# A half of a down projection done at the end of its own group, or at the start of the next

## The chip, the cores and the metric

The kernel runs on one core of one Trainium2 chip. The metric is the device time of one execution in microseconds (us). The kernel before took 368.73 us, the median of three runs (368.56 to 369.21). All times below are from these runs and from one profiled execution of the same kernel.

## The reference, cut to what matters

```python
# gated linear attention, 4 batches x 8 heads x 768 tokens x 48
for t in range(S):
    state = alpha[t][:, None] * state + k[t] (outer) v[t]
    y[t] = q[t] @ state
x = y, heads side by side              # (3072 tokens, 384)
h = x @ w_in                           # 384 -> 1024
u = h * softmax(h)                     # over the 1024
ln = (u - mean(u)) / sqrt(var(u) + 1e-6) * g_ln
out = ln @ w_out                       # 1024 -> 384
```

## The kernel before, in words

**The tiles.** The 768 positions are cut into G = 6 *groups* of 128 positions. A group holds all four batches, so it is 4 x 128 = 512 tokens: N = 24 pieces of 128 tokens, with piece n = 4 g + b. Attention for a group is done in chunked form: decays by scans on VectorE (DVE), scores and read-out as small matmuls on TensorE (PE). The second half of the kernel works on the whole group with features on the partitions:

- `up(g, f)`, for f = 0 to 7, makes 128 of the 1024 hidden features for the 512 tokens: three f32 matmuls of 128x512 into one bank `h` (line 394; the profile counts six rows, two to an f32 matmul). ScalarE (ACT) takes the exponential `e` (line 408), DVE multiplies h by e into `u` (line 409), and ACT squares u (line 412). `running` (line 427) adds e on GpSimd (POOL) and u squared on DVE to running sums `p`. The softmax denominator is never divided out. It cancels in the norm, so only sums over features are needed.
- `down(n, half)` (line 507) multiplies four of the eight feature blocks of one 128-token piece by `w_out` into a bank `o`: four f32 matmuls of 128x385, eight rows in the profile. Half 0 needs u of f = 0 to 3, half 1 that of f = 4 to 7. A piece is complete after both halves, and a pool of two banks holds `o`.
- `finish(n)` (lines 532 to 549) turns a complete `o` into the output: three tiny operations on DVE, a power on POOL (`r`, line 546), a scaled copy on ACT (`o_sb`, line 548), and the output DMA on SyncE's queue.
- `token_sums(g)` (line 462 on) brings the running sums of a group into token order with 16 small matmuls. It waits for `running(g, 7)` on DVE and POOL.

**The order of the work.** The schedule is manual: each engine runs its instructions in the order in which the Python code emits them. The main loop takes g = 1 to 5. Each g has eight steps s = 0 to 7, and in each step the code emits `up(g, s)`, some of the attention of group g + 1 (from a table: `head`, `behind`, `middle`, `tail`), and one half of a down projection from a list `todo`. When that half is a half 1, `finish` of the piece follows after the `up` of the next step, through the variable `after`; for a half 1 in step 7, right at the end of the group.

**The end of a group.** In step 7, `middle` runs `read_values` of group g + 1 (128 rows of matmuls at line 333 that end the read-out `y`, one bank per batch), and then four copies on ACT (line 363) that bring y into `x`, the right operand of the next group's `up`. For the states of groups 3 and 4, `next_state` (line 371, `kv`) follows in the `tail` of step 7; for those of groups 1 and 2 it stands after `up(g, 0)`, and the last group needs none. Between `read_values` and `up(g + 1, 0)` stands the half of a down projection that step 7 takes from `todo`.

**Which half stands where, before.** For g = 1 the list is empty until step 7, where `todo.append((g * B, 0))` puts in half 0 of the group's own first piece, and it runs at once. The other seven halves of the group run in steps 0 to 6 of the next group, and step 7 there again takes the first half of its own group. The last group (g = 5) adds none, so it has no half in step 7. Its eight halves all run after the loop: two of them, then `token_sums(5)` and `last_norm`, then six more with the last checks between them.

Of the kernel before, what the change touches and what calls it, by code (L numbers as in the profile page):

```python
# [32 lines left out]
def fast_path(ctx, tc, q, k, v, alpha, moe_w_in, moe_w_out, moe_g_ln, out):  # L33
# [13 lines left out]
    B, H, S, D = q.shape  # L47
    NTOK, DM = out.shape
    DFF = moe_w_in.shape[1]
    G = S // P  # L50
# [5 lines left out]
    FC = DFF // P  # L56
# [308 lines left out]
    def next_state(g):  # L365
        kv = banks("kv", [H, D], 2)
        for h in range(H):
            for c in range(2):
                for r in range(4):
                    b = 2 * (r // 2) + c  # L370
                    nc.tensor.matmul(
                        kv[c][quarter(r), h], lhsT=kg[:, b, h, E0 * (r % 2) : E0 * (r % 2) + E0],
                        rhs=vn[:, b, HW * h + E1 : HW * h + HW], start=True, stop=True,
                        tile_position=(0, 32 * r), skip_group_check=True,
                    )
        for c in range(2):
            s = held(state, c)
            if g == 0:
                nc.scalar.copy(out=s, in_=kv[c])
            else:  # L380
                nc.vector.tensor_tensor(out=s, in0=s, in1=kv[c], op=ALU.add)
# [4 lines left out]
    def up(g, f):  # L386
        up_mm(g, f)
        up_act(g, f)
# [65 lines left out]
    def token_sums(g):  # L454


        d = gr[g]
        t = ps_a.tile([P, B, 2, 32], FP, tag="a3", name="rows") if g else ps_h.tile([P, B, 2, 32], FP, tag="h", name="rows")
        for b in range(B):
            for r in range(4):  # L460
                c = b * P + 32 * r
                nc.tensor.matmul(
                    t[quarter(r), b], lhsT=d["unit"][:, 0:32], rhs=d["p"][:, :, c : c + 32], start=True, stop=True,
                    tile_position=(0, 32 * r), skip_group_check=True,
                )
        tt = work.tile([P, B, 2, 32], FP, name="cols")
        nc.vector.transpose(out=tt.rearrange("p b i t -> p (b i t)"), in_=t.rearrange("p b i t -> p (b i t)"))
        s = sums[:, g * B : g * B + B]
        nc.vector.tensor_copy(out=s[:, :, 1:3], in_=tt[:, :, :, 0])
        sq = small.tile([P, B], FP, name="sq")  # L470
        nc.vector.tensor_tensor(out=sq, in0=s[:, :, 1], in1=s[:, :, 1], op=ALU.mult)
        d["s"] = small.tile([P, B], FP, name="s")
        nc.vector.scalar_tensor_tensor(
            out=d["s"], in0=sq, scalar=1e-6 * DFF, in1=s[:, :, 2], op0=ALU.mult, op1=ALU.add
        )
# [42 lines left out]
    def finish(n):  # L518
        g, b = divmod(n, B)
        d = st[n]  # L520
        s, whole = sums[:, n], d.get("held", d["o"])
        o = whole[:, 0:DM]
        t0 = b * S + g * P
        if g == G - 1:
            o_sb = work.tile([P, DM], FP, name="o_sb")
            r = gr[g]["r"][:, b : b + 1]
            nc.vector.tensor_scalar(out=o_sb[:, 0:P], in0=o[:, 0:P], scalar1=r, scalar2=None, op0=ALU.mult)  # L527
            nc.scalar.activation(out=o_sb[:, P:DM], in_=o[:, P:DM], func=AF.Copy, scale=r)  # L528
            nc.scalar.dma_start(out=out[t0 : t0 + P, :], in_=o_sb)
            d.clear()  # L530
            return
        nc.vector.tensor_copy(out=s[:, 0:1], in_=whole[:, DM : DM + 1])
        t = small.tile([P, 1], FP, name="t")
        nc.vector.scalar_tensor_tensor(
            out=t, in0=s[:, 0:1], scalar=-1.0 / DFF, in1=s[:, 0:1], op0=ALU.mult, op1=ALU.mult
        )
        nc.vector.tensor_tensor(out=s[:, 3:4], in0=t, in1=gr[g]["s"][:, b : b + 1], op=ALU.add)  # L537
        if g == 0:

            centred = work.tile([P, DM], FP, name="o_mean")  # L540
            nc.vector.scalar_tensor_tensor(
                out=centred, in0=mean_sb, scalar=s[:, 0:1], in1=o, op0=ALU.mult, op1=ALU.add
            )
            o = centred
        r = small.tile([P, 1], FP, name="r")
        nc.gpsimd.tensor_tensor(out=r, in0=s[:, 3:4], in1=mhalf, op=ALU.pow)  # L546
        o_sb = work.tile([P, DM], FP, name="o_sb")
        nc.scalar.activation(out=o_sb, in_=o, func=AF.Copy, scale=r)  # L548
        nc.sync.dma_start(out=out[t0 : t0 + P, :], in_=o_sb)
        d.clear()  # L550
# [110 lines left out]
    def centre(f):  # L661
        nc.gpsimd.tensor_tensor(out=w_out[:, f, 0:DM], in0=w_out[:, f, 0:DM], in1=mean_sb, op=ALU.add)
# [200 lines left out]
    def attend(a, what):  # L863

        more = a + 1 < G
        if what == "v":
            load_v(a)
        elif what == "keys":
            keys_T(a)
            keys(a)  # L870
            if more:
                load(k, kn, a + 1)
        elif what[:2] == "on":
            if what == "on2":
                inverses(a)
            scan_on(a, int(what[2]))
        elif what == "lasts":
            lasts(qn, qe[:, :, 0:P])
            ends_of_decay()
            queries(2)  # L880
            move_lasts()
        elif what == "firsts":
            firsts(qn, qv[:, 0:H, 0:P])
            queries(0)
            queries(1)
            move_firsts()
            if more:
                load(q, qn, a + 1)
        elif what == "apart":
            apart()  # L890
        elif what == "decay":
            decay(a)
        elif what == "keys_back":
            if more:
                keys_back(a)
        elif what[:6] == "scores":
            scores(a, int(what[6]))
        elif what[:6] == "masked":
            masked(int(what[6]))
        elif what == "alpha" and more:  # L900
            alpha_T(a + 1)
            if a > 2:
                attend(a, "over")
        elif what == "over" and more:
            alpha_over(a + 1)
            if a + 2 < G:
                load(alpha, an, a + 2)
        elif what == "back" and more:
            for i in range(3):
                scan_back(a + 1, i)  # L910
        elif what == "begin":
            read_begin()
        elif what[:4] == "read":
            read_state(int(what[4]))
        elif what == "values":
            read_values(a)
        elif what == "kv" and more:
            next_state(a)

    centres = {4: (0, 1), 6: (2, 3), 7: (4, 5, 6, 7)}  # L920
    todo = []
    for g in range(1, G + 1):
        rise, att = g < G, g + 1 < G
        plan = first if g == 1 else usual

        def at(where, s):
            for what in plan[where].get(s, "").split() if att else ():
                attend(g + 1, what)

        after = 3 if g == 1 else None  # L930
        if not rise:
            break
        for s in range(FC):
            at("head", s)
            if rise:
                up(g, s)
            if after is not None:
                finish(after)
                after = None
            if s == 0 and g < 3:  # L940
                next_state(g)
            if s == 0 and g > 1:
                token_sums(g - 1)
            at("behind", s)
            for f in centres.get(s, ()) if g == 1 else ():
                centre(f)
            if rise and s:
                running(g, s)
            at("middle", s)
            if s == FC - 1 and g < G - 1:  # L950
                todo.append((g * B, 0))
            if todo:
                n, half = todo.pop(0)
                down(n, half)
                if half:
                    after = n
            at("tail", s)
        if after is not None:
            finish(after)
        todo = [(n, half) for n in range(g * B, g * B + B) for half in range(2)][g < G - 1 :]  # L960


    for n, half in todo[:2]:
        down(n, half)
        if half == 1:
            token_sums(G - 1)
            last_norm()
    finish(G * B - B)
# [449 lines left out]
def kernel(tc, *args):  # L1418

    with ExitStack() as ctx:  # L1420
        taken = fast_path(ctx, tc, *args)
    with tc.If(taken > 0):
        general_path(tc, *args)
# [30 lines left out]
```

## Time and profile before

| | |
|---|---|
| time, median of three runs | 368.73 us (368.56 to 369.21) |
| the profiled execution: its own time | 369.21 us |
| its span in the profile | 367.4 us |
| instructions | 10036 |
| TensorE busy (matmul rows) | 359.7 us, 98% of the span |
| VectorE, ScalarE, GpSimd busy | 245.4, 146.1, 131.1 us |
| mean granted TensorE clock | 0.998 |
| `down` rows (line 507) | 384, mean 492 ns |
| `up` rows (line 394) | 288, mean 598 ns |
| HBM | 25.30 MB read, 4.72 MB written |

The profiled execution's own time is 1.8 us longer than its span, and 0.48 us longer than the median of the runs. A line of the timeline has the start, the duration, the engine, the source line, the operation and tiles, and the number of rows merged into it. In brackets is the idle time of that engine before it, with the releaser. Durations of matmuls overlap, since they are pipelined, and their ends are modelled: the distance from one start to the next is what counts.

### The profile page before, as it was taken

To read this page: it belongs to the slowest core of one execution; us is meant where nothing else is said; L and a number is where in the kernel's file an instruction comes from. 1 tells how busy PE (TensorE), PEld (TensorE's weight loads), DVE (VectorE), ACT (ScalarE), POOL (GpSimd) and SP (SyncE) were. 2 spreads that over 40 slices of the span, in tenths; PEclk is the share of its full clock that TensorE was granted. 3 is DMA by queue.
4 is the path that set the end of the run, shared out by engine and by line. 5 is a ranking of instruction groups with operands and counts; after the bars stand their busy time and mean duration, and the time that the engine had idled before them with its cause. 6 is when DMAs were issued, how large, how long until landed. Compare 5 with 4: busy or idle time off the path is not lost. (4 is left out here: it accounts for less than half of the span.)

```text
span 367.4 us, 10036 instructions
## 1 busy us (share of the span) xinstructions
PE 359.7 (98%) x4341; PEld 215.9 (59%) x4341; DVE 245.4 (67%) x375; ACT 146.1 (40%) x260; POOL 131.1 (36%) x129
## 2 busy tenths in 40 slices
PE   8999999999999999999999999999999999999994
PEld 8885355676755566566575556574556565555552
DVE  0999999979998787936575935665956314345420
ACT  2647878282645262251432252431242132222110
POOL 7020000004449944763133764232774121233300
PEclk9999999999999999999999999999999999999999
DMA  9996986335196419363135354004042000000011
GB/s 181 186 317 181 220 269 130 87 82 144 53 229 146 105 29 184 77 154 86 33 80 118 75 129 118 4 23 87 21 101 60 2 23 0 24 21 22 23 46 51
DMA packets 72871, 36.06 MB, mean 98 GB/s; under 512 B 48232, under 2 KB 70000, under 8 KB 72816
## 3 DMA queue, kind: packets, MB, share of 16 engines
q1 hardware_dynamic: 71792, 34.39, 39.8%
q10 hardware_dynamic: 1024, 0.92, 0.8%
q8 instruction: 36, 0.59, 0.7%
q14 instruction: 19, 0.16, 0.1%
HBM read 25.30 MB, written 4.72 MB: 82 GB/s over the span
## 5 line engine op out<-in xcount | busy, mean ns | idle before, releaser
L507 PE MATMUL o<-w_out,room 128*128 128x385 f32 x384 | 134.0, 492 | 0.0
L394 PE MATMUL h<-x,w_in 128*128 128x512 f32 x288 | 132.1, 598 | 0.5 <-DVE g_col L642 0.5
L507 PEld LDWEIGHTS o<-w_out,room 128*128 128x128 f32 x384 | 71.0, 190 | 54.7 <-issue 13.1
L394 PEld LDWEIGHTS h<-x,w_in 128*128 128x128 f32 x288 | 52.9, 189 | 58.2 <-issue 49.1
L409 DVE TENSOR_TENSOR room<-h,e 128x512 f32<-128x512 f32 x40 | 27.5, 688 | 73.7 <-ACT e L408 73.7
L408 ACT ACTIVATE e<-h 128x512 f32<-128x512 f32 x40 | 24.0, 599 | 100.6 <-PE h L394 100.6
L427 POOL TENSOR_TENSOR p<-p,e 128x512 f32<-128x512 f32 x30 | 42.7, 1423 | 20.0 <-ACT e L408 19.9
L412 ACT ACTIVATE u<-room 128x512 f32<-128x512 f32 x40 | 25.2, 630 | 39.3 <-DVE room L409 39.3
L546 POOL TENSOR_TENSOR r<-sums,mhalf 128x1 f32<-128x1 f32 x20 | 14.8, 739 | 72.9 <-DVE sums L537 72.7
L289 DVE TENSOR_TENSOR sT<-a,mask 128x512 f32<-128x512 f32 x43 | 26.7, 683 | 7.7 <-PE a L278 7.6
L204 DVE TENSOR_TENSOR_SCAN hT<-aT,unit 128x516 f32<-128x516 f32 x18 | 24.0, 1376 | 8.1 <-ACT aT L703 8.1
L204 DVE TENSOR_TENSOR_SCAN aT<-aT,seed 128x516 f32<-128x516 f32 x18 | 27.4, 1551 | 0.2
L427 DVE TENSOR_TENSOR p<-p,u 128x512 f32<-128x512 f32 x30 | 23.1, 768 | 5.1 <-ACT u L412 5.1
L225 POOL TENSOR_TENSOR kT<-kT,hT 128x1024 f32<-128x1024 f32 (+1 forms) x8 | 14.2, 1796 | 32.6 <-DVE kT L179 32.6
L278 PEld LDWEIGHTS a<-qv,kT 32*128 32x128 f32 x704 | 21.4, 186 | 7.4 <-issue 2.4
L278 PE MATMUL a<-qv,kT 32*128 32x128 f32 x704 | 23.9, 278 | 0.9 <-DVE qv L721 0.4
L212 POOL COPY fend<-hT 128x12 f32<-128x12 f32 x6 | 3.0, 507 | 56.1 <-DVE hT L204 56.1
L333 PE MATMUL y<-sT,vn 128*32 128x128 f32 x768 | 22.6, 273 | 0.2 <-DVE sT L289 0.2
L333 PEld LDWEIGHTS y<-sT,vn 128*32 128x32 f32 x768 | 20.7, 110 | 3.3 <-issue 2.7
L196 ACT ACTIVATE sq<-an,mone 128x1536 uint8<-128x1536 f32 x12 | 18.9, 1573 | 0.2
L548 ACT ACTIVATE o_sb<-o,r 128x384 f32<-128x384 f32 x16 | 9.3, 581 | 18.7 <-POOL r L546 18.7
L261 POOL TENSOR_TENSOR state<-state,lot 128x384 f32<-128x384 f32 x10 | 8.8, 900 | 12.0 <-DMA lot<-qv 11.8
(148 smaller groups left out, 375.8 us busy)
## 6 DMA issues: line engine op xcount, KB each, us to landing
vn<-in_v_dram SPq DMA_DIRECT2D x24, 192.0 KB, 4.6
an<-in_alpha_dram SPq DMA_DIRECT2D x20, 192.0 KB, 3.8
out_dram<-o_sb SPq DMA_DIRECT2D x20, 192.0 KB, 1.9
room<-in_moe_w_out_dram SPq DMA_DIRECT2D x8, 384.0 KB, 5.0
kn<-in_k_dram SPq DMA_DIRECT2D x16, 192.0 KB, 4.8
qn<-in_q_dram SPq DMA_DIRECT2D x16, 192.0 KB, 3.8
lot<-qe SPq DMA_DIRECT2D x40, 64.5 KB, 2.1
lot<-qv SPq DMA_DIRECT2D x20, 129.0 KB, 2.4
```

The source lines that it names most:

```text
L196: nc.scalar.activation(out=sq, in_=x, func=AF.Relu, scale=sign, bias=mone, accum_out=over[:, g, i : i + 1])
L204: nc.vector.tensor_tensor_scan(out=o, data0=a, data1=s, initial=1.0, op0=ALU.mult, op1=ALU.add)
L278: nc.tensor.matmul(a[b][:, i], lhsT=kT[quarter(b), kb], rhs=qv[quarter(b), qb, 0:P], start=not last and not i, stop=bool(last), tile_posit ...
L289: nc.vector.tensor_tensor(out=sT[:, b, half * NP : half * NP + NP], in0=a[b], in1=mask[:, None, :].to_broadcast([P, NP, P]), op=ALU.mult,)
L333: nc.tensor.matmul(y_bank(b)[quarter(r), a], lhsT=lhsT, rhs=rhs, start=(b, r) not in begun, stop=stop, tile_position=(row, 32 * r), skip_g ...
L394: nc.tensor.matmul(h, lhsT=w_in[:, a, f * P : (f + 1) * P], rhs=d["x"][:, a].rearrange("p b t -> p (b t)"), start=(a == 0), stop=(a == KC ...
L408: nc.scalar.activation(out=e, in_=h, func=AF.Exp)
L409: nc.vector.tensor_tensor(out=u, in0=h, in1=e, op=ALU.mult)
L412: nc.scalar.activation(out=u2, in_=u, func=AF.Square)
L427: eng.tensor_tensor(out=p, in0=d[0][i] if f == 1 else p, in1=d[f][i], op=ALU.add)
L507: nc.tensor.matmul(d["o"][:, 0 : DM + 1], lhsT=u_of(g, f)[:, b * P : b * P + P], rhs=w_out[:, f], start=(f == 0), stop=(f == FC - 1), skip ...
L546: nc.gpsimd.tensor_tensor(out=r, in0=s[:, 3:4], in1=mhalf, op=ALU.pow)
```

## The change

The step in which a group's own first half is put into step 7 is taken out, and the list of the next group is no longer shortened by it. All eight halves of group g now run in steps 0 to 7 of group g + 1. Every half of groups 1 to 4 runs one step later. Step 7 of group 1 has no half, and step 7 of group 5 has one: half 1 of piece 19. After the loop, `token_sums` and `last_norm` stand after one half instead of two. `finish` moves with its half: from steps 1, 3, 5 and 7 to steps 2, 4, 6 and the end of step 7. No instruction's shape and no amount of arithmetic is changed.

```diff
@@ main loop, step s of group g
             at("middle", s)
-            if s == FC - 1 and g < G - 1:
-                todo.append((g * B, 0))
             if todo:
                 n, half = todo.pop(0)
                 down(n, half)
@@ end of group g
         if after is not None:
             finish(after)
-        todo = [(n, half) for n in range(g * B, g * B + B) for half in range(2)][g < G - 1 :]
+        todo = [(n, half) for n in range(g * B, g * B + B) for half in range(2)]
 
     for n, half in todo[:2]:
         down(n, half)
-        if half == 1:
+        if half == 0:
             token_sums(G - 1)
             last_norm()
     finish(G * B - B)
```

## The prediction

> **What bounds the kernel now.** I read the page first (busy times, then the 40 slices), then TensorE's timeline from the first group to the end, then ScalarE's and VectorE's around the end of group 1, and last all engines around the end of group 2.
>
> The page, sections 1 and 2:
>
> ```profile
> PE 359.7 (98%) x4341; PEld 215.9 (59%) x4341; DVE 245.4 (67%) x375; ACT 146.1 (40%) x260; POOL 131.1 (36%) x129
> ...
> PE   8999999999999999999999999999999999999994
> ```
>
> PE has work in every slice but the first and last. A table of windows gives 87.70 us of PE rows in 30 to 118 us, and rows without a gap in each window I took between 118 and 346 us. So the time is the sum of PE's blocks, and other engines matter only where they make PE wait. Now PE around the end of group 1, and its end:
>
> ```profile
> 128.21 3.70 PE L333 MATMUL y<-sT,vn 128*32 128x128 f32 x128
> 131.84 2.86 PE L507 MATMUL o<-w_out,room 128*128 128x385 f32 x8
> 134.54 2.74 PE L394 MATMUL h<-x,w_in 128*128 128x512 f32 x6
> 137.21 1.57 PE L371 MATMUL kv<-vn,kg 128*32 128x48 f32 x128
> 138.59 0.64 PE L462 MATMUL rows<-p,ones 128*32 128x64 f32 x32
> 139.16 2.86 PE L507 MATMUL o<-w_out,room 128*128 128x385 f32 x8
> ...
> 340.19 5.35 PE L507 MATMUL o<-w_out,room 128*128 128x385 f32 x16
> 345.47 0.65 PE L462 MATMUL rows<-p,ones 128*32 128x64 f32 x32
> 345.94 0.48 PE L485 MATMUL rows_u<-lot,ones 128*32 128x32 f32 x32
> 346.35 8.04 PE L507 MATMUL o<-w_out,room 128*128 128x385 f32 x24
> ```
>
> The row at 131.84 is the half that the change moves away. The row at 134.54 is `up(2, 0)`, which reads x. ScalarE in the same place:
>
> ```profile
> 131.98 0.48 ACT L363 COPY x<-y 128x384 f32<-128x384 f32 x1 [0.39 <-PE y L333]
> 132.36 1.58 ACT L196 ACTIVATE sq<-an,mone 128x1536 uint8<-128x1536 f32 x1
> ...
> 135.54 0.19 ACT L196 ACTIVATION_READ_ACCUMULATOR sq<-an,mone 128x1 f32 x1
> 137.37 0.60 ACT L408 ACTIVATE e<-h 128x512 f32<-128x512 f32 x1 [1.64 <-PE h L394]
> ```
>
> The fourth copy starts 0.07 us after y's modelled end (128.21 + 3.70 = 131.91) and ends at 132.46. The moved half covers it fully: `up` begins 2.08 us after x is there.
>
> **The end of group 1.** Without the half, PE goes from the last row of y to `up(2, 0)`, which waits for the fourth copy: 132.46, plus the time for PE to wake. The nearest rows for that: a VectorE result of 17.95 starts matmuls at 18.00, and one of 28.84 at 28.90 (0.05 to 0.06 us); a mask of 23.26 (the first of two merged rows, halved) starts weight loads at 23.37 (0.11). This instruction waits for two engines, so I take 0.11: PE restarts at 132.57. Were x ready, it would start at 131.84, where the half starts now. The stall costs 0.73 us (bounds 0.67 and 0.75).
>
> `up` after a stall takes a little longer to its next block: the one that began at 28.90 after a wait reached `kv` at 31.65, 2.75 us, while the one at 134.54, after a full block of `down`, took 2.67. That is 0.08 more (bounds 0 and 0.10, the 2.77 of an `up` between two y blocks in group 2). The half taken out spans 131.84 to 134.54, 2.70 us.
>
> Hence `kv` begins at 132.57 + 2.75 = 135.32 where it was 137.21: PE is 1.89 us ahead here.
>
> **The next wait in line.** `token_sums(1)` needs the running sum of f = 7. VectorE in this place:
>
> ```profile
> 131.67 4.32 DVE L204 TENSOR_TENSOR_SCAN hT<-aT,unit 128x516 f32<-128x516 f32 x3
> 135.92 0.66 DVE L427 TENSOR_TENSOR p<-p,u 128x512 f32<-128x512 f32 x1
> 138.00 0.69 DVE L409 TENSOR_TENSOR room<-h,e 128x512 f32<-128x512 f32 x1 [1.43 <-ACT e L408]
> ```
>
> The sum ends at 136.58 and does not move with PE, for VectorE works without a pause up to it. `rows` would start at 135.32 + 1.38 (`kv` to `rows` now) = 136.70; 136.58 plus 0.11 is 136.69. So the cover is gone here too, but just enough: I take nothing, with a bound of 0.2 above (the three scans took 4.51 us at the end of group 2, not 4.32). After it, ScalarE is free of its two range checks at 135.73, 0.24 us after h is ready (135.32 plus the 0.17 from `kv`'s start to e at 137.37 less 137.21). That delays e(2, 0) by 0.24 us against PE, and no PE block needs it before `up(2, 2)`, two `up`s and two halves later, which reuses the bank.
>
> **The rest of the loop, groups 2 to 5.** Each step has one half as before, only another one, so PE's blocks are the same in kind and order. Half 0 and half 1 cost the same: a pair of `up` and `down` takes 5.17 us throughout. What moves is `finish`. In steps 2, 4 and 6 its three VectorE operations (0.5 us) stand behind the scans of step 1 and ahead of the transposes of steps 2 and 6, and its POOL power (0.74 us mean) ahead of the copies and products of the queries. The first o bank is asked for again only two steps later, 8 us or more. Of the queries' products, the last ended at 213.89 and the scores began at 219.86: 6 us of cover for a delay under 1 us. On SyncE's queue the output DMA of a group's last piece now stands ahead of four loads of v, which wait with it for about 3.5 us; v is read only in step 7. These are nothing, under that cover.
>
> At the end of step 7, `finish` of the fourth piece now stands behind `next_state`. Group 2 shows what it meets:
>
> ```profile
> 187.21 0.58 ACT L548 ACTIVATE o_sb<-o,r 128x384 f32<-128x384 f32 x1 [1.31 <-POOL r L546]
> ...
> 187.69 1.61 ACT L363 COPY x<-y 128x384 f32<-128x384 f32 x4
> ...
> 190.23 1.57 PE L371 MATMUL kv<-vn,kg 128*32 128x48 f32 x128
> ...
> 191.81 1.02 DVE L381 TENSOR_TENSOR state<-state,kv 128x384 f32<-128x384 f32 x2 [1.11 <-PE kv L371]
> ...
> 194.61 0.60 ACT L408 ACTIVATE e<-h 128x512 f32<-128x512 f32 x1 [5.30 <-PE h L394]
> ```
>
> The state sums end at 192.83, the three operations near 193.4, the power between 193.95 and 194.8 (0.55 to 1.41 us in the rows), and o_sb 0.58 later, at 194.6 to 195.4. So e(3, 0), queued behind it on ScalarE, and u behind e, come 0 to 0.8 us late. The bank they hold is wanted by `up` two steps on, at 202.95, while u ended at 195.93. Nothing, with 6 us of cover.
>
> **The end.** Step 7 of group 5 gets a half, and after the loop one half instead of two stands ahead of `token_sums(5)`: 16 rows from `up(5, 7)` to `rows`, as now. The half is more behind it: 32 rows in place of the 24 at 346.35. Those took 7.97 us to the next block at 354.32, 2.66 a half (the 16 ahead of `rows` 5.28, 2.64 a half). I take 2.66 us. The norm of the last group is then covered by seven halves instead of six.
>
> **The sum.** 0.73 (stall) + 0.08 (start) - 2.70 (half out) + 2.66 (half in) = +0.77 us. On the profiled execution: 369.21 + 0.77 = 369.98; on the median of the runs, 0.48 lower, 369.50. I predict 369.5 us. This kernel's measurement can tell about 0.2%, 0.74 us, from no change, and the forecast lies on that line.
>
> [...] PE's clock stays at 1.00 in the windows across the gaps I could find: 0.30 us idle at 113.37, and PE's idle 0.45 us ahead of `up(0, 0)` at 28.90. So I charge 0.7 us of idle no clock. [...] The first weight load of `up(0, 0)` came at 28.87, only after the wait. [...]
>
> **Rivals.**
>
> *A wait per group* (12%). The o_sb behind `next_state` holds ScalarE, and PE waits where it uses h or the running sums. For: it stands ahead of e in a strict order. Against: the 6 us above. At 0.8 us for each of three group ends (2 to 3, 3 to 4, 4 to 5) it gives 2.4 + 0.77, 371.9 us. It decides once the power ends later than about 200 instead of 194.8.
>
> *The tight `rows`* (14%). VectorE's chain is later than 136.6, and PE waits 0.2 to 0.7 us more at `token_sums(1)`: 369.7 to 370.2 us. It speaks for it that the margin I work out is 0.01 us.
>
> *Faster* (6%). At the ends of groups 2 to 4, o_sb no longer stands ahead of x's copies. Now the fourth copy ends at 187.69 + 1.61 = 189.30; it could end at 188.1, 1.2 us sooner. If the copies set when `kv` and `up` begin there, three ends would give 3.6, and the time were 368.73 + 0.77 - 3.6 = 365.9. It decides if x is late for PE; but `kv` starts at 190.23, 0.9 us after the last copy, with no gap ahead of it.
>
> *Nothing* (8%). The stall is partly filled: `up` starts with its weights loaded and at the short wake, and the extra half at the end falls on time that is hidden there. +0.2 to +0.5 us, 369.0 to 369.2.
>
> **How the numbers follow.** The forecast has 60%, with +0.63 (0.67 + 0 - 0.04) to +1.01 (0.75 + 0.10 - 0.04 + 0.2) us, 369.4 to 369.7, and a scatter of the median of 0.2. Some 35 of it fall over the 0.2% line, 25 within. With the two slower rivals: slower 0.61. Within: 25 + 8 = 0.33. Faster 0.06. The range takes in *nothing* at its low end and the tight `rows` at its high end: 369.0 to 370.4; the group waits and the gain, 18% together, lie outside.
>
> **What would show it.** Right: PE idle of about 0.7 us ahead of line 394 near 132, released by ACT x; `kv` near 135.3; the 16 rows of line 507 that follow `up(5, 7)` near 338.3, and 32 rows after `rows_u`; `rows` of group 1 with no or a short wait; the same 55.9 us from `up(3, 0)` to `up(4, 0)` as now. Wrong: PE waits ahead of line 394 or 462 in groups 3 to 5, a clock below 1.00 after 132, or no gap at 132.

## The result, and the profile after

The changed kernel took 370.12 us (median of 4 runs, 369.71 to 370.72), against 368.81 us before (4 runs): a ratio of 1.0036 with a 95% interval of 1.0018 to 1.0053. In a later comparison with more runs the same program took 370.11 us (8 runs) against 368.97 us (25 runs), a ratio of 1.0029 (1.0017 to 1.0041), which is 1.1 us. So it is slower by some 0.3%. The forecast of 369.5 us was right in sign and place and 0.6 us too low; the cost forecast, 0.77 us, stands against 1.3 and 1.1 us measured.

The page, sections 1 and 2, of the changed kernel (span 368.9 us):

```profile
PE 359.6 (97%) x4341; PEld 215.7 (58%) x4341; DVE 244.8 (66%) x375; ACT 146.6 (40%) x260; POOL 124.4 (34%) x129
...
PE   8989999999999999999999999999999999999994
```

TensorE's busy time is the same (359.7 before), in a span that is 1.5 us longer. So the change added no work; it added idle time. The page cannot show where. TensorE's timeline at the end of group 1 and around the end of the loop does:

```profile
128.85 3.70 PE L333 MATMUL y<-sT,vn 128*32 128x128 f32 x128
133.16 2.84 PE L394 MATMUL h<-x,w_in 128*128 128x512 f32 x6 [0.60 <-ACT x L363]
135.93 1.57 PE L371 MATMUL kv<-vn,kg 128*32 128x48 f32 x128
137.49 0.65 PE L462 MATMUL rows<-p,ones 128*32 128x64 f32 x32
138.08 2.86 PE L507 MATMUL o<-w_out,room 128*128 128x385 f32 x8
...
339.11 5.35 PE L507 MATMUL o<-w_out,room 128*128 128x385 f32 x16
344.39 0.65 PE L462 MATMUL rows<-p,ones 128*32 128x64 f32 x32
344.86 0.48 PE L485 MATMUL rows_u<-lot,ones 128*32 128x32 f32 x32
345.26 10.64 PE L507 MATMUL o<-w_out,room 128*128 128x385 f32 x32
```

The row of line 507 after the read-out is gone, and the next row carries a gap with its releaser: 0.60 us until x. At the end, 32 rows stand where 24 stood. The last row of line 507 shown, with the half that came in, takes 10.57 us to the next block instead of 7.97. Between the two places, groups 2 to 5 run as before: `up(3, 0)` to `up(4, 0)` takes 55.92 us in both traces (190.64 to 246.56 here).

**Spans of single traces mislead here.** The read-out of group 2 (the row at 128.85) is the last block ahead of the first changed instruction. It begins at 128.21 us in the trace of before, and at 128.85 us in this one, though the instructions up to it are the same. In this trace POOL's decay of the state, ahead of it, waited 1.14 us for a DMA of the queries, where before it did not:

```profile
121.91 2.09 POOL L261 TENSOR_TENSOR state<-state,lot 128x384 f32<-128x384 f32 x2 [1.14 <-DMA lot<-qv]
```

TensorE waited 0.57 us for that state, most of the 0.64. A second trace of the same changed program has its read-out at 127.70 us. So this part moves by itself by up to 1.15 us. I therefore compare stretches: A is the start of that read-out, B the start of the single matmul `all_ok` near the end, the same instruction in every variant.

| kernel | A, us | A to B, us | B to end, us | against before, A to B |
|---|---|---|---|---|
| before, two traces | 128.21, 127.99 | 226.11, 226.13 | 13.1, 13.3 | |
| changed, two traces | 128.85, 127.70 | 226.98, 227.23 | 13.1, 13.2 | +0.9, +1.1 |

### The profile page after: what moved, and what is told of

It reads as the page before. It is cut to its first block, busy times and chain, and to the rows that moved or that the text cites. A ratio compares the mean times of both kernels' runs of the same rounds, so it can differ in the third digit from the quotient of the medians.

```text
span 368.9 us, 10039 instructions
## 1 busy us (share of the span) xinstructions
PE 359.6 (97%) x4341; PEld 215.7 (58%) x4341; DVE 244.8 (66%) x375; ACT 146.6 (40%) x260; POOL 124.4 (34%) x129
## 5 line engine op out<-in xcount | busy, mean ns | idle before, releaser
L427 POOL TENSOR_TENSOR p<-p,e 128x512 f32<-128x512 f32 x30 | 41.5, 1383 | 26.7 <-ACT e L408 26.4
L546 POOL TENSOR_TENSOR r<-sums,mhalf 128x1 f32<-128x1 f32 x20 | 12.7, 637 | 75.9 <-DVE sums L537 75.7
L289 DVE TENSOR_TENSOR sT<-a,mask 128x512 f32<-128x512 f32 x43 | 26.7, 684 | 13.2 <-PE a L278 13.2
L427 DVE TENSOR_TENSOR p<-p,u 128x512 f32<-128x512 f32 x30 | 24.4, 813 | 7.2 <-ACT u L412 7.2
L212 POOL COPY fend<-hT 128x12 f32<-128x12 f32 x6 | 4.0, 668 | 55.9 <-DVE hT L204 55.9
L363 ACT COPY x<-y 128x384 f32<-128x384 f32 x24 | 11.2, 477 | 7.0 <-PE y L333 6.7
```

The source lines that it names most:

```text
L289: nc.vector.tensor_tensor(out=sT[:, b, half * NP : half * NP + NP], in0=a[b], in1=mask[:, None, :].to_broadcast([P, NP, P]), op=ALU.mult,)
L427: eng.tensor_tensor(out=p, in0=d[0][i] if f == 1 else p, in1=d[f][i], op=ALU.add)
```

## The experiments

Theory A: only the end of group 1 costs, in two waits that stand in a row, first x's last copy and then the running sum that `token_sums(1)` needs. Theory B: the time lies elsewhere, in the later `finish` of every group or in the part ahead of the change.

**The changed kernel again** (`e1_after`, no edit).

> The changed kernel again, for a narrower interval and a second trace. In its first trace, the stretch from read_values at the end of group 1 to the end costs 0.87 us more than before; another 0.64 us lies ahead of the first changed instruction, where a DMA of the queries landed late. Theory A (only the end of group 1 costs): +0.9 us against the kernel before, and a trace in which the part ahead of the change varies by itself. Theory B (the late finish of every group, or the part ahead of the change, costs lastingly): +1.3 us.

Ratio 1.0029 (1.0017 to 1.0041), A to B +1.1 us. TensorE's timeline shows both waits:

```profile
132.01 2.84 PE L394 MATMUL h<-x,w_in 128*128 128x512 f32 x6 [0.61 <-ACT x L363]
134.78 1.57 PE L371 MATMUL kv<-vn,kg 128*32 128x48 f32 x128
136.59 0.65 PE L462 MATMUL rows<-p,ones 128*32 128x64 f32 x32 [0.25 <-DVE p L427]
```

The first is as long as in the first trace, the second is longer: `kv` to `rows` takes 1.81 us against 1.56 there and 1.38 before. VectorE, in the same trace, says why:

```profile
131.13 4.73 DVE L204 TENSOR_TENSOR_SCAN hT<-aT,unit 128x516 f32<-128x516 f32 x3
135.79 0.66 DVE L427 TENSOR_TENSOR p<-p,u 128x512 f32<-128x512 f32 x1
```

The three scans ahead of the sum took 4.73 us here, 4.45 in the first changed trace and 4.32 in the first trace of before. The change does not cause this: the second trace of before has 4.44. The interval alone does not separate +0.9 from +1.3; the traces put 0.9 to 1.1 at this place.

**The before kernel again** (`e7_before`, no edit).

> The kernel before again: 0 us, an interval that shows what the comparison can tell, and a second trace of the part ahead of the change. Theory A: that part varies between traces of the same instructions by some tenths of a us.

Ratio 0.9999 (0.9990 to 1.0008), A at 127.99 us. So 0.1% can be told from no change here, and the part ahead of A varies without any edit.

**Cover for x alone** (`e2_kv`): `next_state(2)` goes ahead of `up(2, 0)`.

```diff
-        tail={6: "begin read0"},
+        tail={6: "begin read0", 7: "kv"},
...
-            if s == 0 and g < 3:
+            if s == 0 and g < 2:
                 next_state(g)
```

> Changed kernel with next_state(2) moved ahead of up(2, 0), so that its 1.5 us cover the last copy of x. Theory A says that two waits stand in a row: the copy of x, and then token_sums(1) on the running sum. Taking away the first alone lets TensorE reach token_sums sooner, only to wait there: no idle ahead of line 394, about 0.6 to 0.8 us idle ahead of line 462, and the same time as the changed kernel, +0.7 to +0.9 us against before. Rival (the stall on x is the whole cost): 0.0 to +0.2 us against before.

```profile
131.26 1.66 PE L371 MATMUL kv<-vn,kg 128*32 128x48 f32 x128
132.85 2.84 PE L394 MATMUL h<-x,w_in 128*128 128x512 f32 x6
136.41 0.65 PE L462 MATMUL rows<-p,ones 128*32 128x64 f32 x32 [0.72 <-DVE p L427]
```

Ratio 1.0024 (1.0014 to 1.0034), A to B 227.00 us, +0.9. The gap ahead of line 394 is gone and stands ahead of line 462 instead, 0.72 us long. Taking away the stall that the prediction priced brings nothing by itself: the sum is late in the same place. The rival, that x is the whole cost, falls.

**Cover for the sum alone** (`e3_sums`): `token_sums(1)` goes behind the half of step 0.

```diff
-            if s == 0 and g > 1:
+            if s == 0 and g > 2:
                 token_sums(g - 1)
...
                 down(n, half)
                 if half:
                     after = n
+            if s == 0 and g == 2:
+                token_sums(g - 1)
```

> Changed kernel with token_sums(1) moved behind the half of step 0 of group 2, so that the running sum has 2.7 us more. Theory A: the 0.18 us at line 462 goes, the 0.6 us at line 394 stays: +0.7 us against before. Rival (token_sums is the main wait): 0 to +0.2 us.

Ratio 1.0028 (1.0018 to 1.0039), A to B 227.12 us, +1.0. The gap of 0.60 us ahead of line 394 stays, and there is none ahead of line 462, but I expected +0.7 and the time did not fall. TensorE's timeline:

```profile
134.98 1.57 PE L371 MATMUL kv<-vn,kg 128*32 128x48 f32 x128
136.48 2.86 PE L507 MATMUL o<-w_out,room 128*128 128x385 f32 x8
139.27 0.65 PE L462 MATMUL rows<-p,ones 128*32 128x64 f32 x32
139.85 2.84 PE L394 MATMUL h<-x,w_in 128*128 128x512 f32 x6
```

The move itself costs what it saves: `kv`, `rows` and `down` together take 4.65 us before (137.21 to 141.86) and, in the new order and without any wait, 4.87 us (134.98 to 139.85 in this trace). The `up` behind them takes 2.68 us to the next block instead of 2.57. These 0.33 us belong to the order alone. So this run takes the second wait away, but by itself it does not show that the wait cost anything.

**Both** (`e4_both`): the two edits together.

> Both moves in one. Theory A: no gap at either place, and the time of the kernel before within 0.2 us (0.0 to +0.2). Theory B (late finish or the part ahead of the change): still +0.5 to +1.3 us.

Ratio 1.0006 (0.9997 to 1.0015), 369.22 us against 368.97: not told from no change. A to B is 226.84 us, of which 0.47 us is one gap inside `kv`:

```profile
131.75 0.84 PE L371 MATMUL kv<-vn,kg 128*32 128x48 f32 x58
133.07 0.97 PE L371 MATMUL kv<-vn,kg 128*32 128x48 f32 x70 [0.47 <-issue]
```

Gaps put down to "issue", 0.47 to 0.83 us long, also stand in five other traces, one of them of the before kernel, all near 24 us, ahead of A. What causes them is open. Without it the stretch is an estimated 226.37, +0.25 us, in which the dearer order of `e3_sums` is contained. So two covers give back nearly all that the change took, where each alone gives nothing that shows: in `e2_kv` because the second wait took the place of the first, in `e3_sums` because the first stayed and the order cost 0.33 us. The two waits stand in a row. Theory B falls with this, since this kernel keeps every later `finish` and the later halves.

**The step without a half at another place.** In two kernels only groups up to 1, or up to 3, run a half in their own step 7, so that the empty step is that of group 2, or of group 4.

```diff
-            if s == FC - 1 and g < G - 1:
+            if s == FC - 1 and g <= 1:          # the other kernel: g <= 3
                 todo.append((g * B, 0))
...
-        todo = [(n, half) ...][g < G - 1 :]
+        todo = [(n, half) ...][g <= 1 :]
...
-        if half == 1:
+        if half == 0:
             token_sums(G - 1)
```

> Only group 1 runs its first half in its own step 7; the step without a half is then step 7 of group 2, where next_state follows the read-out at once. Theory A, by ScalarE's queue: there o_sb of the piece before stands ahead of x's copies, and next_state needs the banks of the first two copies, which end near 188.55 in the trace of before, 1.1 us after the read-out: line 371 idles 1.1 us, and the time is +1.0 us against before. Rival (next_state covers the copies): 0 us. Theory B (late finish in groups 2 to 5): three quarters of the whole change, +0.7 to +1.0 us, without a gap at line 371.

`e5_upto1`: ratio 1.0023 (1.0012 to 1.0033), A to B 227.01 us, +0.9. TensorE and ScalarE at the end of group 2:

```profile
187.76 0.58 ACT L548 ACTIVATE o_sb<-o,r 128x384 f32<-128x384 f32 x1 [1.31 <-POOL r L546]
188.24 1.61 ACT L363 COPY x<-y 128x384 f32<-128x384 f32 x4
188.76 1.86 PE L371 MATMUL kv<-vn,kg 128*32 128x48 f32 x128 [0.70 <-ACT x L363]
190.56 2.84 PE L394 MATMUL h<-x,w_in 128*128 128x512 f32 x6
```

`kv` waits for the first copies, which stand behind o_sb on ScalarE. The gap is 0.70 us, not 1.1: `kv` begins when about the first of the four copies is done, and it then takes 1.80 us to the next block where it took 1.50 before. Together it is the 1.0 us expected.

> Groups 1 to 3 run their first half in their own step 7; the step without a half is step 7 of group 4, where up(5, 0) follows the read-out at once. Theory A: o_sb stands ahead of the copies, the last of which ends near 299.03 in the trace of before: line 394 idles 1.1 us, +1.2 us against before. Rival (a step without a half costs the 0.7 us of one copy wherever it is): +0.8 us. Theory B (late finish per group): a quarter of the whole change, +0.2 to +0.3 us.

`e6_upto3`: ratio 1.0033 (1.0022 to 1.0045), A to B 227.23 us, +1.1. Here `up(5, 0)` follows the read-out at once, and the gap is 1.05 us:

```profile
296.95 0.58 ACT L548 ACTIVATE o_sb<-o,r 128x384 f32<-128x384 f32 x1 [0.46 <-POOL r L546]
297.43 1.61 ACT L363 COPY x<-y 128x384 f32<-128x384 f32 x4
299.09 2.84 PE L394 MATMUL h<-x,w_in 128*128 128x512 f32 x6 [1.05 <-ACT x L363]
```

**The same with o_sb out of the way** (`e10_finish`): as `e6_upto3`, with the `finish` in step 7 of group 4 emitted behind the read-out.

```diff
-            if after is not None:
+            if after is not None and (g, s) != (4, 7):
                 finish(after)
                 after = None
...
             at("middle", s)
+            if after is not None and (g, s) == (4, 7):
+                finish(after)
+                after = None
```

> The kernel with groups 1 to 3 as before (no half in step 7 of group 4), with finish of piece 15's forerunner in step 7 of group 4 emitted behind the read-out and x's copies instead of ahead of them. If ScalarE's queue sets the price of a step without a half: the copies end 0.5 us after the read-out, line 394 idles 0.6 us instead of 1.05, and the time is +0.7 us against before instead of +1.2. Rival (the price lies elsewhere, in the halves' order): +1.2 us as without it.

```profile
296.59 1.32 ACT L363 COPY x<-y 128x384 f32<-128x384 f32 x3
298.30 0.48 ACT L363 COPY x<-y 128x384 f32<-128x384 f32 x1 [0.39 <-PE y L333]
298.68 0.59 ACT L548 ACTIVATE o_sb<-o,r 128x384 f32<-128x384 f32 x1
298.84 2.84 PE L394 MATMUL h<-x,w_in 128*128 128x512 f32 x6 [0.60 <-ACT x L363]
```

Ratio 1.0023 (1.0012 to 1.0033), 369.75 us against 368.91, A to B 226.79, +0.7. The gap is 0.60 us, as at the end of group 1 in the changed kernel. So at the end of group 4 a step without a half costs the wait for the last copy of x, and 0.45 us more where another operation stands ahead of the copies on ScalarE.

**A long gap** (`e8_long`): the changed kernel with two extra range checks of alpha ahead of the copies, which change no result.

```diff
-        middle={7: "read1 values over"},
+        middle={7: "read1 over2 values over"},   # over2: alpha_over(a + 1) twice
```

> Changed kernel with two more range checks of alpha (four activations, 6.7 us, no change of the result) ahead of x's copies in step 7 of group 1, so that TensorE idles for about 5.8 us. If idle time costs only itself: +5.0 us against the changed kernel, the granted clock stays 1.00 and the up rows after the gap stay near 592 ns. If an idle stretch of this length halves the clock: a clock below 1.00 after the gap, rows near 1.0 us for some 3 us, and 1.5 to 3 us more.

One run, 376.94 us. The table of windows of this run, TensorE only (us, busy time and rows, granted clock, DMA share, GB/s):

```profile
132.00:137.20 5.20, 0.00 (x0) 0.79 0.00 0
137.20:139.80 2.60, 2.53 (x3) 0.50 0.00 0
139.80:142.30 2.50, 2.50 (x4) 0.59 0.26 65
142.30:146.00 3.70, 3.70 (x167) 1.00 1.07 223
```

The gap was 5.59 us. In windows of 0.05 us the clock is 1.00 up to 135.00 and 0.50 from 135.05 to 141.85: it fell 3.4 us into the gap, stayed low for 6.8 us, and came back 4.6 us after TensorE had work again. `up(2, 0)` took 5.04 us to the next block (137.27 to 142.31) instead of 2.67, its rows up to 1.22 us long, so 2.4 us came on top of the idle time.

**A gap of 2 us** (`e9_mid`): the range check that stands behind the copies goes ahead of them.

```diff
-        middle={7: "read1 values over"},
+        middle={7: "read1 over values"},
```

> Changed kernel with the range check of alpha (two activations, 3.4 us, that stand behind x's copies now) ahead of them in step 7 of group 1, so that TensorE idles for about 2.3 us instead of 0.6. In the run with 5.6 us idle the granted clock fell to half and up(2, 0) took 5.04 us to the next block instead of 2.7. If a gap of this length leaves the clock alone: up(2, 0) takes 2.75 us, the clock stays 1.00, and the run is 1.5 us over the changed kernel (1.7 more idle, less the 0.2 at token_sums). If it halves the clock already: 2.4 us more than that.

One run, 373.03 us, A to B 230.08.

```profile
134.00 4.54 PE L394 MATMUL h<-x,w_in 128*128 128x512 f32 x6 [2.18 <-ACT x L363]
138.47 1.57 PE L371 MATMUL kv<-vn,kg 128*32 128x48 f32 x128
```

```profile
131.82:134.00 2.18, 0.00 (x1) 1.00 0.19 40
134.00:134.50 0.50, 0.50 (x1) 1.00 1.04 346
134.75:138.00 3.25, 3.25 (x5) 0.50 0.69 141
138.25:142.00 3.75, 3.75 (x166) 1.00 0.27 51
```

A gap of 2.18 us was followed by a lower clock too. It was 1.00 through the whole gap and fell at 134.73 (by windows of 0.05 us), 0.7 us after TensorE had work again. It stayed at 0.50 until 138.14, for 3.4 us, half the 6.8 us of `e8_long`. `up(2, 0)` took 4.47 us, 1.8 more than before. After the 1.05 us of `e6_upto3` the clock did not fall: `up(5, 0)` took 2.77 us (299.09 to 301.86).

## Why the prediction was right, and where it was too small

**The place and the sign** were right. TensorE had no idle time to give back, the half at the end of group 1 was cover, and the cost is at that place. The groups behind it kept their length: from `rows` of group 1 to B the time grew by 2.60 us, the same 2.60 that the half which came in takes at the end (10.57 instead of 7.97). The time itself, 370.12 us, lies above the 369.4 to 369.7 that the forecast's own sum gave; the stated range held it because it took in the rival *the tight `rows`*.

**The sum, term by term**, from the two changed traces. The stall, from where the half began to where `up(2, 0)` now begins: 4.31 us after A in both, where the half began 3.63 after A. That is 0.68, predicted 0.73: TensorE started 0.05 to 0.06 us after the last copy, and the 0.11 us taken for an instruction that waits for two engines was too much. The slower start of `up`: 2.77 instead of 2.67, 0.10, predicted 0.08. The size is right, but the stall is not shown to be its cause, see below. The half out: 2.70. The half in: `rows` of group 1 to B grew from 215.74 to 218.34, 2.60, predicted 2.66, since the mean of the three was used and a further half takes less. These four make 0.68 + 0.10 - 2.70 + 2.60 = 0.68 us, against 0.77.

**The mis-sized term** is the next wait in line. The prediction found it, worked out a margin of 0.01 us, and took it at nothing with 0.2 as the bound. It measured 0.18 and 0.43 us (1.56 and 1.81 from `kv` to `rows` instead of 1.38). With it the sum is 0.86 and 1.11, which is the A to B of the two traces (+0.86 and +1.11 against the mean of before). The margin was worked out with scans of 4.32 us, and there luck came in: of the twelve traces of these experiments, in all of which these three scans are the same work, it has the shortest. Six others have 4.44 to 4.47 us, five 4.69 to 4.79; the mean is 4.56, so a quarter of a us would have been the better estimate. The bound of 0.2 was set by a trio of 4.51 us, the one at the end of group 2 in that same trace, and was too small as well. The wake was a smaller error: from the end of the sum to `rows` it took 0.14 us in both traces, not 0.11. The rival *the tight `rows`*, at 14%, was the nearest to what came: 369.7 to 370.2.

**The rest of the loop** was right to be put at nothing. o_sb behind `next_state` was feared to delay e(3, 0) by up to 0.8 us. In the trace it ended at 193.43, just before h was ready, and e started without a wait for it:

```profile
192.85 0.58 ACT L548 ACTIVATE o_sb<-o,r 128x384 f32<-128x384 f32 x1 [5.88 <-POOL r L546]
193.52 0.60 ACT L408 ACTIVATE e<-h 128x512 f32<-128x512 f32 x1
```

*A wait per group*, *faster* and *nothing* did not come. The observation behind *faster*, o_sb ahead of the copies, is real and cost 0.45 us in `e6_upto3`; but before the change a half of a down projection covered it.

**The clock** was rightly left out for a gap of 0.6 us: it is 1.00 in the window from 133.2 to 140 us. The gaps of 0.30 and 0.45 us on which the prediction rested this said nothing of longer ones: in `e9_mid` a gap of 2.18 us was followed by a clock of 0.50.

**The start of `up`.** The rival *nothing* let `up` start with its weights loaded. It did not: after the stall the first weight load of `up(2, 0)` starts with the first matmul, at 133.16, where before it started at 134.22, 0.32 us ahead of it. But the stall need not be the reason. In the trace of before, `up(3, 0)` follows `kv` with no wait, its first weight load starts with its first matmul too, at 191.73, and it also takes 2.77 us to the next block. So in these places: behind a `down` the first load starts 0.32 us ahead of the first matmul (134.22 and 141.54 in the trace of before, 140.46 in the changed one), while behind matmuls of the read-out (124.35 before) or `kv` (191.73 before) it starts with it, with no wait ahead.

**What stays open.** The first comparison gave +1.3 us, the later one +1.1, and the stretch shows 0.9 and 1.1. The rest is within the scatter of the part ahead of A, but two traces cannot show that it is nothing else. That the scans' length varies by almost 0.5 us is measured; what slows them was not tried.

## What to carry to other kernels

When one engine has no idle time, ask of each block that is moved what it was covering, and then who is next: here a second wait stood just behind the first, so that a cover for the first alone only moved the idle time, while both covers together gave back nearly everything. A margin of 0.01 us read from one trace is no margin: price it with the spread of that chain over several traces. Compare stretches between two instructions that both kernels have, since the part ahead of a change can differ by more than the change costs.

## What the runs showed of the hardware

The granted clock of TensorE fell to 0.50 at a gap of 5.59 us, 3.4 us into it (`e8_long`, 2.4 us lost on one `up`), and at one of 2.18 us, 0.7 us after TensorE was at work again (`e9_mid`, 1.8 us lost), one run each. It stayed low for 6.8 and 3.4 us. After the gap of 0.60 us in the changed kernel and that of 1.05 us in `e6_upto3` it was 1.00. What a gap between 1.05 and 2.18 us does, and whether it matters when the gap falls or what TensorE ran ahead of it, no run shows.

The order of blocks of different shapes had a price of its own in `e3_sums`: the same `kv`, `rows` and `down` took 4.87 us in another order instead of 4.65, and the `up` behind them 2.68 instead of 2.57, with no wait in it. And three scans of 128x516 on VectorE took 4.32 to 4.79 us at the same place in twelve traces.
